# Attention and a gated FFN on one core: another order for the weight steps, the late block, the pairs' first pass and their second steps

## The chip, the cores and the metric

The kernel runs on one core of a Trainium2 chip. The metric is the time of one execution in microseconds of the device. Five engines share the work: TensorE (PE in the profile; PEld is its loading of weights), VectorE (DVE), ScalarE (ACT), GpSimd (POOL) and SyncE (SP). SP does nothing but issue DMAs, one after the other in its own order.

## The reference

Attention inside chunks of 64 positions, for each batch and head, and then a gated feed-forward network over all tokens:

```python
scores = scale * np.matmul(q_c, k_c.transpose(0, 1, 2, 4, 3))      # 64 x 64 in each chunk
attn = np.exp(scores - max) ; attn = attn / (attn.sum + 1e-09)
x = np.matmul(attn, v_c)                                            # as 4608 tokens x 512
g = x @ w_gate ; val = x @ w_val                                    # 512 x 1536 each
out = (g / (1 + np.exp(-g)) * val) @ w_out                          # 1536 x 512
```

There are 8 batches, 8 heads and 576 positions of 64. The inputs q, k, v are float32; the three weights arrive as 64-bit floats and are narrowed on the chip.

## The kernel before, in words

**Tiling.** The 4608 tokens are nine blocks of 512, the 1536 columns twelve steps f of 128. A float32 product is made of three matmuls: each operand is split into an upper and a lower part (`split`: ACT copies the upper, DVE subtracts for the lower), and lower x upper, upper x lower and upper x upper are summed. A step of one block is thus a gate and a value product of 12 matmuls of 128x512 each, Silu of the gate on ACT (`silu`, L490), the product with the value on DVE (`times`, L497), the split of that h (`parts`), and the projection (`project`, L516 to L518) of four row tiles with three matmuls each, summed over all f in four banks of PSUM (`ps_o`). `lag` holds a projection back by one step.

**Stages.** *Opening* (0 to 47 us): attention and the first step of blocks 0 and 1 (a0, a1), a written-out list. *Weight steps* f = 1 to 10 (47 to 196): per step gate and value of a0, the projection of f - 1, gate and value of a1, 60 matmuls. Beside them the weights of the next step are prepared: `Up` for gate and value weights, `Out` for output weights, by `scale` and `below` on ACT and `shift`, `power`, `weigh`, `join` on DVE; `Quarters` forms sums of the up weights for the pairs (`sums`, and then `upper` and `lower`, a split), and the results are stored to DRAM (`save_w`, `save_o`, `quarters.save`). Block 1's h goes to DRAM as well (`put_off`). *Late part* (196 to 259): f = 11, and then block 1's twelve projections, from h and output weights read back (`prepare`, `out_again`), in the order 0 to 11, with the attention of block 2 beside it (`extra`). *Block 2* (259 to 380): twelve direct steps of 36 matmuls, and behind each a piece (`behind`) of the attention of blocks 3 and 4 or of the quarters of weights 0 and 1 (`redo`). *Pairs* (3,4), (5,6) and (7,8): `both_steps` computes gate and value of both blocks by seven products of 6 matmuls in place of eight (`seventh`, L952; factors are the quarters and weights read back by `load_weights`) and the first block's projections, one row tile at each `turn_of`; `second_steps` then makes the second block's twelve projections of 12 matmuls. Behind them stands the attention of the next pair: scores, `exponents` and `normalize`, `turn` (transposes on DVE), `load_v`, `values`, and the next pair's operands `x0` to `x6`.

**Order.** On PE, ACT and DVE the instructions run as the code is written (`manual_schedule`, L543). On SP that holds up to the end of f = 11 (`loading`); from there the scheduler chooses the order of the DMA issues. A tile name with a tag has a fixed place: a new tile of the same tag waits until the old one's readers are done. Output weights read back share the three places of `wp`.

## Time and profile before

| | us |
|---|---|
| median of 3 runs | 980.46 (979.53 to 981.21) |
| the profiled execution | 979.93 |
| its span | 978.1 |
| PE busy in it | 915.6 |
| DVE busy | 550.2 |
| ACT busy | 367.7 |
| moved by DMA | 221.17 MB |

A row of waits names the engine and tile that waited, then what ended the wait, then total us, count and the longest. In a timeline a row begins with its time and its length in us; a bracket gives the idle time ahead of it and what ended it. In the issues the last column is the us from issue to landing.

### The profile page before, as it was taken

What the parts mean: (1) busy time and instruction counts of PE and PEld (TensorE: products, weight loads), DVE (VectorE), ACT (ScalarE), POOL (GpSimd) and SP (SyncE); (2) the same over time, 40 slices, a digit from 0 to 9 for tenths busy, and PEclk for the clock granted to TensorE, in tenths of its full rate; (3) what the DMA queues carried; (4) which work ended last, traced back from release to release, by engine and by line L of the source; (5) the groups of instructions that cost most, each with busy time, mean ns of one, the idle gap of its engine ahead of it and who ended that gap; (6) DMA issues with size and microseconds to landing.
All of it is one profiled execution on the core that took longest, in us unless ns stands there. A gap on an engine that the chain in (4) does not pass through costs nothing.

```text
span 978.1 us, 14802 instructions
## 1 busy us (share of the span) xinstructions
PE 915.6 (94%) x6083; PEld 746.8 (76%) x6083; DVE 550.2 (56%) x863; ACT 367.7 (38%) x561; POOL 6.1 (1%) x14
## 2 busy tenths in 40 slices
PE   7998898887979999999999889999999899999988
PEld 6877677776867877878877668788787688888876
DVE  6976776753377576567586252685673533333332
ACT  4754454441432324342333433423424342222222
POOL 1100000000000000000000000000000000000000
PEclk9999999998998999999999999999999899999999
DMA  9678677769672554765555875656557556555345
GB/s 360 251 293 299 259 253 299 269 237 318 237 220 97 167 211 162 275 242 219 193 200 214 289 252 188 243 215 237 203 208 228 171 200 239 214 215 212 134 151 172
DMA packets 73315, 221.17 MB, mean 226 GB/s; under 512 B 30752, under 2 KB 31008, under 8 KB 59552
## 3 DMA queue, kind: packets, MB, share of 16 engines
q1 hardware_dynamic: 71520, 217.08, 61.8%
q10 hardware_dynamic: 1728, 3.15, 0.9%
q8 instruction: 48, 0.79, 0.3%
q14 instruction: 19, 0.16, 0.0%
HBM read 176.16 MB, written 44.04 MB: 225 GB/s over the span
## 4 chain that ended last, share of the span: by engine, by line
PE 62%; ACT 5%; DVE 5%; DMA 4%; issue 3%; SPq 1%; DVEq 0%; ACTq 0%
PE ps_a L952 20%; PE ps_gv L952 14%; PE ps_o L516 7%; PE ps_o L517 7%; PE ps_o L518 7%; PE ps_gv L461 4%; DMA both<-o 2%; DVE turned L338 1%; PE ps_a L273 1%; ACT s_sb L294 1%; DMA v_t<-in_v 1%; DVE hl L65 1%; ACT hh L64 1%; SPq L255 1%; ACT x L64 1%
## 5 line engine op out<-in xcount | busy, mean ns | idle before, releaser
L952 PE MATMUL ps_a<-x,factors 128*128 128x512 f32 x864 | 220.4, 390 | 5.1 <-ACT h L973 5.1
L516 PE MATMUL ps_o<-both,hl 128*128 128x512 f32 x432 | 173.1, 401 | 22.7 <-DMA both<-o 14.4
L952 PEld LDWEIGHTS ps_a<-x,factors 128*128 128x128 f32 x864 | 161.5, 188 | 40.6 <-ACT h L973 7.2
L461 PE MATMUL ps_gv<-xh,w 128*128 128x512 f32 x576 | 180.2, 397 | 0.0
L517 PE MATMUL ps_o<-both,hh 128*128 128x512 f32 x432 | 170.8, 395 | 0.0
L518 PE MATMUL ps_o<-both,hh 128*128 128x512 f32 x432 | 170.6, 395 | 0.0
L952 PE MATMUL ps_gv<-x,factors 128*128 128x512 f32 x648 | 164.8, 390 | 0.0
L952 PEld LDWEIGHTS ps_gv<-x,factors 128*128 128x128 f32 x648 | 121.3, 188 | 26.5 <-issue 1.5
L461 PE MATMUL ps_gv<-xl,w 128*128 128x512 f32 x288 | 114.5, 404 | 19.9 <-ACT h L490 18.1
L461 PEld LDWEIGHTS ps_gv<-xh,w 128*128 128x128 f32 x576 | 110.8, 192 | 23.4 <-ACT xh L591 0.2
L516 PEld LDWEIGHTS ps_o<-both,hl 128*128 128x128 f32 x432 | 82.7, 191 | 44.4 <-issue 11.6
L65 DVE TENSOR_TENSOR hl<-h,hh 128x512 fp32r<-128x512 f32 x96 | 65.7, 688 | 82.2 <-ACT hh L64 82.2
L64 ACT CAST hh<-h 128x512 fp32r<-128x512 f32 x96 | 58.9, 616 | 106.2 <-PE ps_o L518 59.9
L518 PEld LDWEIGHTS ps_o<-both,hh 128*128 128x128 f32 x432 | 82.7, 191 | 17.8
L517 PEld LDWEIGHTS ps_o<-both,hh 128*128 128x128 f32 x432 | 83.0, 192 | 16.9
L338 DVE STREAM_TRANSPOSE turned<-s_sb 32x256 f32<-32x256 f32 x192 | 83.7, 436 | 2.5
L461 PEld LDWEIGHTS ps_gv<-xl,w 128*128 128x128 f32 x288 | 55.3, 192 | 36.1 <-ACT h L490 22.7
L956 DVE TENSOR_TENSOR h<-h,ps_gv 128x512 f32<-128x512 f32 x36 | 24.7, 687 | 102.9 <-PE ps_gv L952 97.8
L497 DVE SCALAR_TENSOR_TENSOR h<-v,h 128x512 f32<-128x512 f32 x72 | 49.8, 692 | 43.9 <-ACT h L990 39.8
L990 ACT ACTIVATE h<-ps_a 128x512 f32<-128x512 f32 x36 | 21.5, 598 | 110.9 <-PE ps_a L952 110.9
L981 ACT ACTIVATE h<-h 128x512 f32<-128x512 f32 x36 | 22.8, 632 | 75.0 <-DVE h L956 75.0
L490 ACT ACTIVATE h<-ps_gv 128x512 f32<-128x512 f32 x36 | 21.4, 595 | 60.7 <-PE ps_gv L461 60.7
(99 smaller groups left out, 725.8 us busy)
## 6 DMA issues: line engine op xcount, KB each, us to landing
both<-o SPq DMA_DIRECT2D x96, 512.0 KB, 4.9
factors<-w SPq DMA_DIRECT2D x36, 1024.0 KB, 4.8
factors<-t SPq DMA_DIRECT2D x36, 1024.0 KB, 6.2
w<-w SPq DMA_DIRECT2D x12, 1024.0 KB, 4.9
t<-th SPq DMA_DIRECT2D x12, 1024.0 KB, 6.4
raw<-in_wgv SPq DMA_DIRECT2D x11, 1024.0 KB, 10.3
qk_t<-in_qk SPq DMA_DIRECT2D x10, 1024.0 KB, 7.4
out<-o_sb SPq DMA_DIRECT2D x35, 256.0 KB, 3.2
```

The lines of the kernel that those rows point to most:

```text
L64: nc.scalar.copy(out=hi, in_=src)
L65: (engine or nc.vector).tensor_tensor(out=lo, in0=src, in1=hi.bitcast(F32), op=ALU.subtract)
L338: nc.vector.transpose(out=self.turned[to:to + 32, p:p + 2, j, :, 32 * (i % 2):32 * (i % 2) + 32], in_=src[32 * i:32 * i + 32, :, o // 2, 3 ...
L461: nc.tensor.matmul(ps, w, x, start=first and (k, i) == which[0], stop=last and (k, i) == which[-1])
L497: nc.vector.scalar_tensor_tensor(out=h, in0=pv, scalar=2.0 ** -8, in1=h, op0=ALU.mult, op1=ALU.mult)
L516: nc.tensor.matmul(o, hl[:, ts], woh, start=f == 0, stop=False)
L517: nc.tensor.matmul(o, hh[:, ts], wol, start=False, stop=False)
L518: nc.tensor.matmul(o, hh[:, ts], woh, start=False, stop=f == NF - 1)
L952: nc.tensor.matmul(ps, w[:, u, k], x[:, v, k], start=first and k == 0 and n == 0, stop=k == NK // 2 - 1 and n == 2, skip_group_check=True)
L956: nc.vector.tensor_tensor(out=t, in0=t, in1=ps, op=ALU.add)
L981: nc.scalar.activation(h, h, AF.Silu, scale=2.0 ** -8)
L990: nc.scalar.activation(h2, ps1, AF.Silu, scale=2.0 ** -8)
```

## The change

*Weight steps.* `sums` stands behind `join`; the second Silu stands ahead of the quarters' copy and of `scale` of the next output weights; the quarters' lower part behind that. The output weights' store is issued at the step's begin and the quarters' store ahead of the next output weights' load. The quarters of weight 1 are formed at the end of the opening, those of weight 0 in the late part; `redo` is gone. *Late part.* Block 1's last two steps (10 and 11) are not put off to DRAM but projected first (`a1.steps`); the others follow, their output weights in five places in turn, two of them the tags wo0 and wo1. *Output weights in DRAM* lie two steps together, so that one transfer (`out_of_two`) brings two. *Pairs.* In steps 1, 5, 8 and 11 (`bursts`) only the first row tile is projected inside; five products run behind each other, then a row tile, scores or values, and the last two row tiles. Exponents stand in the middle of steps 2 and 6. The sums of `x1`, `x2`, `x5` become steps of their own (`s1`, `s2`, `s4`, `s5`). v1 and v2 lie in one tile under the tags ts and wo1. *Second steps.* All weights are asked for at once, steps 2 to 9 two by two; the next pair's factors are loaded behind step 6 and step 10, and both `values` lie in `both_steps`.

```diff
-            wo_raw.append(const.tile([P, DM], F32, name="wo", tag=f"wo{self.f % 4}"))
+            wo_raw.append(const.tile([P, 2, DM], F32, name="wo", tag=f"wo{self.f % 2}")[:, 0])
...
-        kept_o[f] = store.tile([P, 2, DM], F32, name=f"o{f}")
+        if f % 2 == 0:
+            o = store.tile([P, 2, 2, DM], F32, name=f"o{f}")
+            kept_o[f], kept_o[f + 1], two_o[f // 2] = o[:, 0], o[:, 1], o
         out_now[f] = both
         return both[:, 0], both[:, 1]
...
-    def out_again(f):
-        both = wp.tile([P, 2, DM], F32R, name="both", tag="wo")
+    def out_again(f, pool=wp, tag="wo"):
+        both = pool.tile([P, 2, DM], F32R, name="both", tag=tag)
         nc.sync.dma_start(out=both.bitcast(F32), in_=kept_o[f])
         return both[:, 0], both[:, 1]
...
+    def out_of_two(f, tag):
+        two = const.tile([P, 2, 2, DM], F32R, name="two", tag=tag)
+        nc.sync.dma_start(out=two.bitcast(F32), in_=two_o[f // 2])
+        return [(two[:, i, 0], two[:, i, 1]) for i in range(2)]
...
-            nc.tensor.matmul(o, hl[:, ts], woh, start=f == 0, stop=False)
+            nc.tensor.matmul(o, hl[:, ts], woh, start=f == a.steps[0], stop=False)
...
-            nc.tensor.matmul(o, hh[:, ts], woh, start=False, stop=f == NF - 1)
-            if f == NF - 1:
+            nc.tensor.matmul(o, hh[:, ts], woh, start=False, stop=f == a.steps[1])
+            if f == a.steps[1]:
...
     o.join()
+    quarters = Quarters(1)
+    quarters.sums(w.t)
     p0 = parts(a0, 0, h0)
     wo_f = out_weights(0)
     lag(p0, wo_f)
     down[1].load()
     down[1].scale()
...
+    quarters.upper()
+    quarters.lower()
...
     for f in range(1, NF - 1):
         w, o = up[f + 1], down[f]
+        save_o(f - 1)
         if f + 2 < NF:
             up[f + 2].load()
-        save_o(f - 1)
+        quarters.save()
         down[f + 1].load()
-        if quarters:
-            quarters.save()
         quarters = Quarters(f + 1)
         h0 = gate(a0, f)
...
         w.lower()
-        quarters.sums(w.t)
         o.weigh()
         o.join()
+        quarters.sums(w.t)
         if f + 2 < NF:
             up[f + 2].scale()
-        down[f + 1].scale()
-        quarters.upper()
         wo_f = out_weights(f)
         lag(p0, wo_f)
+        h1 = gate(a1, f)
+        quarters.upper()
+        down[f + 1].scale()
         quarters.lower()
-        h1 = gate(a1, f)
         pv1 = value(a1, f)
...
+    def fetch_h(i):
+        if i < NF // 2 - 1:
+            h = ld.tile([P, 2, N], F32, name="h_in", tag="qk_t")
+            nc.sync.dma_start(out=h, in_=kept_h[i])
+            late.append(h)
     def prepare(f):
-        if f % 2 == 0:
-            h = ld.tile([P, 2, N], F32, name="h_in", tag="qk_t")
-            nc.sync.dma_start(out=h, in_=kept_h[f // 2])
-            late.append(h)
-        p = parts(a1, f, late[-1][:, f % 2])
-        return p, out_again(f)
+        p = parts(a1, f, late[f // 2][:, f % 2])
+        if f % 2:
...
+    ready_o = []
+    def fetch_o(n):
+        while len(ready_o) < min(n, NF - 2):
+            f = len(ready_o)
+            ready_o.append(out_again(f, const, f"wo{f % 5 - 1}") if f % 5 in (1, 2) else out_again(f))
...
-    wo_f = out_weights(f)
+    last_o, wo_f = wo_f, out_weights(f)
     lag(p0, wo_f)
+    a1.steps = f - 1, f - 2
+    put = [(parts(a1, f - 1, h1), last_o)]
     nxt.less_top(nxt.products([nxt.load_qk(2, 2, const, "turned")]), 2)
     h1 = gate(a1, f)
-    put = [prepare(0)]
+    fetch_h(0)
+    fetch_o(1)
     lag(None, None)
-    put.append(prepare(1))
+    fetch_h(1)
+    fetch_o(2)
     save_o(f - 1)
-    quarters.save()
-    save_o(f)
     pv1 = value(a1, f)
     times(h1, pv1)
-    put_off(h1)
+    put.append((parts(a1, f, h1), wo_f))
     loading.__exit__(None, None, None)
...
     nxt.places()
-    extra = {0: lambda: nxt.exponents(0), 1: lambda: (nxt.exponents(2), sums(0)), 2: lambda: nxt.normalize(0, z[0]),
-             3: lambda: (sums(2), load_v()), 4: lambda: nxt.normalize(2, z[2]), 6: turn, 7: lambda: copy(2),
-             8: columns, 9: lambda: (first(2), rest(0)), 10: lambda: rest(2)}
+    extra = {0: lambda: (nxt.exponents(0), quarters.save()), 1: lambda: (nxt.exponents(2), sums(0)), 2: lambda: nxt.normalize(0, z[0]),
+             3: lambda: (sums(2), load_v()), 4: lambda: nxt.normalize(2, z[2]), 5: lambda: (q0.sums(q0.again()), q0.upper()),
+             6: lambda: (turn(), q0.lower(), q0.save()), 7: lambda: copy(2), 8: columns, 9: lambda: (first(2), rest(0)), 10: lambda: rest(2)}
+    save_o(NF - 1)
     for f in range(NF):
         lag(*put.pop(0))
+        fetch_o(f + 3)
         extra.get(f, lambda: None)()
         if f + 2 < NF:
-            put.append(prepare(f + 2))
+            put.append((prepare(f), ready_o[f]))
...
+        def s1(self):
             self.sum = ld.tile([P, NK // 2 * N], F32, name="sum", tag="qk_t")
             nc.vector.tensor_tensor(out=self.sum, in0=self.quarter(1, 0), in1=self.quarter(1, 1), op=ALU.add)
+        def x1(self):
             self.halves(1, self.sum)
...
+    def turns(which):
+        if pending:
+            project(*pending[0], which=which)
+            if T - 1 in which:
+                pending.pop()
...
             wo_f = out_again(f)
-            h = gated_pair(pair, f, kept[-1][:, f % 2])
+            h = gated_pair(pair, f, kept[-1][:, f % 2], [0] if f in bursts else range(T),
+                           middle.get(f, nothing))
             p = parts(pair.a[0], f, h)
+            if f in bursts:
+                turns([1])
+                bursts[f]()
+                turns([2, 3])
...
-            lag(p, wo_f)
-            if not (pair.last and f + 2 >= NF):
-                load_weights((f + 2) % NF)
...
     def second_steps(pair, behind, nothing=lambda: None):
-        put = [(parts(pair.a[1], f, pair.kept[f // 2][:, f % 2]), out_again(f)) for f in range(2)]
+        def prepare(f):
+            return parts(pair.a[1], f, pair.kept[f // 2][:, f % 2])
+        wo_f = [out_again(0), out_again(1)]
+        for f in (2, 4, 6, 8):
+            wo_f += out_of_two(f, f"w{6 + f // 2}")
+        put = [prepare(0)]
         for f in range(NF):
-            lag(*put.pop(0))
+            lag(put.pop(0), wo_f[f])
+            if f == 0:
+                wo_f += out_again(10), out_again(11, const, "wo0")
+            if f + 1 < NF:
+                put.append(prepare(f + 1))
             behind.get(f, nothing)()
-            if f + 2 < NF:
-                put.append((parts(pair.a[1], f + 2, pair.kept[(f + 2) // 2][:, f % 2]), out_again(f + 2)))
+            if not pair.last and f in (6, 10):
+                load_weights(f // 10)
...
     a, pair = nxt, Pair(3, "w2")
     c = pair.a[0]
-    first = {0: Quarters(0), 1: Quarters(1)}
-    def redo(f):
...
-    behind = {0: lambda: (redo(0), scores(c, False)), 1: lambda: (softmax_and_turn(c, 0), redo(1)),
+    behind = {0: lambda: scores(c, False), 1: lambda: softmax_and_turn(c, 0),
               2: lambda: (softmax_and_turn(c, 1), softmax_and_turn(c, 2)),
-              3: lambda: (softmax_and_turn(c, 3), load_v(c)), 4: lambda: values(c), 5: lambda: scores(pair.second(), False),
-              6: lambda: softmax_and_turn(pair.a[1], 0),
+              3: lambda: (softmax_and_turn(c, 3), load_v(c)), 4: lambda: (values(c, False), pair.x0(), pair.x3()),
+              5: lambda: scores(pair.second(), False), 6: lambda: softmax_and_turn(pair.a[1], 0),
               7: lambda: (softmax_and_turn(pair.a[1], 1), softmax_and_turn(pair.a[1], 2)),
               8: lambda: (softmax_and_turn(pair.a[1], 3), load_v(pair.a[1]), load_weights(0)),
-              9: lambda: (values(pair.a[1]), pair.x0(), pair.x1()), 10: lambda: (pair.x2(), pair.x3()),
-              11: lambda: (pair.x4(), pair.x5(), load_weights(1), pair.x6())}
+              9: lambda: (values(pair.a[1], False), pair.s1(), pair.x1(), pair.s4()),
...
-                      3: lambda: (softmax_and_turn(c, 1), softmax_and_turn(c, 2)), 4: lambda: softmax_and_turn(c, 3),
-                      6: lambda: scores(n.second()), 7: lambda: softmax_and_turn(n.a[1], 0),
-                      8: lambda: (softmax_and_turn(n.a[1], 1), softmax_and_turn(n.a[1], 2)),
-                      9: lambda: (softmax_and_turn(n.a[1], 3), load_v(c))}
-            later = {0: lambda: values(c), 1: lambda: (load_v(n.a[1]), n.x0()), 3: lambda: (values(n.a[1]), n.x1()),
-                     4: lambda: n.x2(), 6: lambda: n.x3(), 7: lambda: n.x4(), 8: lambda: n.x5(), 10: lambda: n.x6()}
-        both_steps(pair, behind)
+            bursts = {1: lambda: scores(c), 5: lambda: scores(n.second()), 8: lambda: values(c),
+                      11: lambda: values(n.a[1])}
+            middle = {2: lambda: c.exponents(0, NP), 6: lambda: n.a[1].exponents(0, NP)}
+            behind = {2: lambda: c.normalize(0, NP), 3: lambda: (softmax_and_turn(c, 1), softmax_and_turn(c, 2)),
+                      4: lambda: softmax_and_turn(c, 3), 6: lambda: (n.a[1].normalize(0, NP), load_v(c)),
+                      7: lambda: (softmax_and_turn(n.a[1], 1), softmax_and_turn(n.a[1], 2)),
+                      8: lambda: (softmax_and_turn(n.a[1], 3), load_v(n.a[1]))}
+            later = dict(enumerate((n.x0, n.s1, n.x1, n.s4, n.s2, n.x2, n.x3, n.x4, n.s5, n.x5, n.x6)))
+        both_steps(pair, middle, behind, bursts)```

PE's, ACT's and DVE's instructions are the same in number and shape. Three places, as the program orders them.

ACT in a weight step, before (raw is a loaded weight, ts and th the quarters, wo and both the output weights):

```order
L84 ACTIVATE t<-raw 128x1024
L84 ACTIVATE wo<-raw 128x512
L172 CAST th<-ts 128x1024
L64 CAST both<-wo 128x512
L490 ACTIVATE h<-ps_gv 128x512 x2
L555 DMA h_736<-h 128x512
```

and after:

```order
L84 ACTIVATE t<-raw 128x1024
L64 CAST both<-wo 128x512
L500 ACTIVATE h<-ps_gv 128x512
L172 CAST th<-ts 128x1024
L84 ACTIVATE wo<-raw 128x512
L500 ACTIVATE h<-ps_gv 128x512
L565 DMA h_969<-h 128x512
```

The first Silu and the split of the output weights now stand ahead of the quarters' copy and of the scaling of the next output weights.

SP at the start of the first pair's second steps, before (o_711, o_783 and o_896 are the output weights of steps 0, 1 and 2; factors the next pair's):

```order
L477 DMA both<-o_1909 128x1024
L943 DMA factors<-w_2373 128x2048
L943 DMA factors<-t_2443 128x2048
L477 DMA both<-o_711 128x1024
L943 DMA factors<-w_2533 128x2048
L943 DMA factors<-t_2601 128x2048
L477 DMA both<-o_783 128x1024
L477 DMA both<-o_896 128x1024
```

and after (o_715 is that of steps 0 and 1, o_899 to o_1560 those of 2 to 9, two by two, o_1777 that of 10 and 11):

```order
L481 DMA both<-o_1777 128x1024
L487 DMA two<-o_899 128x2048
L487 DMA two<-o_1119 128x2048
L481 DMA both<-o_715 128x1024
L487 DMA two<-o_1339 128x2048
L487 DMA two<-o_1560 128x2048
L255 DMA v_t<-in_v 128x4x64
L257 DMA v_t<-in_v 64x4x64 x2
L255 DMA v_t<-in_v 128x4x64
L257 DMA v_t<-in_v 64x4x64 x2
L247 DMA qk_t<-in_qk 128x2x1024
L481 DMA both<-o_715 128x1024
```

The factors are gone from ahead of the output weights, and the second load from o_715, that of step 1, stands behind six loads of v and one of q and k.

PE in the step of a pair that has scores, from the second row tile on, before:

```order
L952 MATMUL ps_gv<-x,factors 128x512 x6
L516 MATMUL ps_o<-both,hl 128x512
L517 MATMUL ps_o<-both,hh 128x512
L518 MATMUL ps_o<-both,hh 128x512
L952 MATMUL ps_a<-x,factors 128x512 x6
L516 MATMUL ps_o<-both,hl 128x512
L517 MATMUL ps_o<-both,hh 128x512
L518 MATMUL ps_o<-both,hh 128x512
L273 MATMUL ps_a<-qk_t 64x64 x64
```

and after:

```order
L988 MATMUL ps_a<-x,factors 128x512 x6
L988 MATMUL ps_gv<-x,factors 128x512 x6
L988 MATMUL ps_a<-x,factors 128x512 x6
L988 MATMUL ps_gv<-x,factors 128x512 x6
L988 MATMUL ps_a<-x,factors 128x512 x6
L526 MATMUL ps_o<-both,hl 128x512
L527 MATMUL ps_o<-both,hh 128x512
L528 MATMUL ps_o<-both,hh 128x512
L275 MATMUL ps_a<-qk_t 64x64 x64
```

The row tiles that stood between the products stand behind them, and the scores have a row tile ahead of them and two behind.

56 lines of the change are left out of this document (29 added, 27 removed).

## The prediction

> **What bounds the kernel now.** I read the page first, then busy time by stage, then TensorE's waits stage by stage, then single waits in the timeline. The page's span and its first part:
>
> ```profile
> span 978.1 us, 14802 instructions
> PE 915.6 (94%) x6083; PEld 746.8 (76%) x6083; DVE 550.2 (56%) x863; ACT 367.7 (38%) x561; POOL 6.1 (1%) x14
> ```
>
> TensorE (PE) is the bound, and its instructions are the same in number and shape after the change. So only the 62 us in which it stands, and what a stand costs afterwards, can move. Two stages by busy time:
>
> ```profile
> core 0: us, PE busy (x) PEld busy (x) DVE busy (x) ACT busy (x) POOL busy (x), PEclk, DMA share, GB/s
> 47.00:196.00 149.00, 135.83 (x581) 109.06 (x579) 107.93 (x166) 72.18 (x97) 0.00 (x0) 0.99 0.74 278
> 786.00:936.00 150.00, 149.89 (x660) 123.84 (x660) 49.35 (x74) 45.42 (x78) 0.00 (x0) 1.00 0.52 193
> ```
>
> The last pair's first pass (second row) has no stand at all, at a granted clock of 1.00: a denser program is not clocked down. The waits of PE in seven windows, in this order: 47 to 196 (first row), 196 to 259 (next two), 259 to 380 (three), 380 to 536 (one), 536 to 585 (three), 741 to 786 (three), 786 to the end (last):
>
> ```profile
> PE ps_gv L461 <- ACT h L490: 12.6, 9, 2.6
> PE ps_o L516 <- DMA both<-o: 6.8, 1, 6.8
> PE ps_o L516 <- DVE z L427: 1.6, 1, 1.6
> PE ps_gv L461 <- ACT h L490: 4.9, 1, 4.9
> PE ps_gv L461 <- ACT s_sb L281: 1.8, 1, 1.8
> PE ps_a L351 <- DVE h L497: 1.5, 1, 1.5
> PE ps_a L952 <- ACT h L973: 3.5, 3, 1.8
> PE ps_o L516 <- DMA both<-o: 5.4, 2, 3.4
> PE ps_a L351 <- DMA v_t<-in_v: 1.7, 2, 1.4
> PE ps_o L516 <- DVE hl L65: 1.3, 1, 1.3
> PE ps_o L516 <- DVE hl L65: 2.7, 2, 1.3
> PE ps_o L516 <- DMA both<-o: 2.2, 1, 2.2
> PE ps_a L351 <- DMA v_t<-in_v: 1.5, 2, 0.8
> PE ps_o L516 <- ACT o_sb L531: 1.2, 1, 1.2
> ```
>
> What a wait costs beyond its idle time shows in PE's timeline of one weight step:
>
> ```profile
> 84.48 0.61 PE L461 MATMUL ps_gv<-xh,w 128*128 128x512 f32 x2
> 87.71 0.53 PE L461 MATMUL ps_gv<-xl,w 128*128 128x512 f32 x1 [2.61 <-ACT h L490]
> 88.04 1.05 PE L461 MATMUL ps_gv<-xh,w 128*128 128x512 f32 x2
> ```
>
> Two matmuls take 0.61 us warm and 1.05 behind this wait. One starts each 0.227 us (0.61 less one 0.39 row), 0.43 in the slow stretch; eight at half rate add 1.6 us, and the refill 0.16 to every wait. Counted so in PE's timeline, 8 matmuls of the weight stage run at half rate, 7 of the late part, 19 of block 2, 15 of pair 1's second steps and 10 of pair 2's, each 0.2 us lost.
>
> A page of the Trainium skill differs here: "TensorE: Matmul & The Clock Gate", Part 1, lets the clock fall after an idle window of about 3.4 us. The trace does not agree, since 2.61 us was enough. By the page's rule the new 2.1 us wait below would cost no half rate, and the forecast would be 0.8 us lower.
>
> **The change part by part.** *Weight steps, f = 1 to 10.* One step of a sum is 60 matmuls, 13.6 us of PE. In the step around that wait, ACT's timeline, and then DVE's:
>
> ```profile
> 83.01 0.68 ACT L84 ACTIVATE wo<-raw 128x512 f32<-128x512 f32 x1 [2.31 <-DMA raw<-in_wo]
> 85.59 1.04 ACT L172 CAST th<-ts 128x1024 fp32r<-128x1024 f32 x1 [1.91 <-DMA t<-th]
> 87.06 0.59 ACT L490 ACTIVATE h<-ps_gv 128x512 f32<-128x512 f32 x1
> ```
>
> ```profile
> 81.76 0.69 DVE L165 TENSOR_TENSOR ts<-t 128x512 f32<-128x512 f32 x1
> 83.73 0.69 DVE L102 TENSOR_TENSOR wo<-wo,o_sb 128x512 f32<-128x512 f32 x1
> 87.80 1.22 DVE L175 TENSOR_TENSOR th<-ts,th 128x1024 fp32r<-128x1024 f32 x1
> ```
>
> The Silu that frees PE's bank (87.06) stands behind two instructions that wait for transfers, the load of the next output weights and the store of the last quarters. After the change it stands before both, behind only the split of the output weights. The three quarter sums begin at 81.76 and fill, with a 0.4 us product, the 2.0 us to join at 83.73; behind join, they let it start at 82.2 and end at 82.9. Split 0.6, Silu 0.6: done by 84.2, and PE wants the bank at 84.9 (end of the 84.48 row). Margin 0.7 us. DVE then does sums (1.5), the split's lower part (0.7), the quarters' lower part (1.22) and the product of the other block (0.7), to about 87.4 with hand-overs, where PE asks for that at 84.9 + 12 x 0.227 = 87.6. Margin 0.2: next to nothing, and if lost it comes back each step. Gain: 13.2 us idle (with one of 0.6 at 196), ten refills, one half rate: 16.4.
>
> Against it: the quarters of weight 1 now stand in the opening on DVE, ahead of the product that PE's value product waits for:
>
> ```profile
> 42.55 0.68 DVE L65 TENSOR_TENSOR hl<-h,hh 128x512 fp32r<-128x512 f32 x1
> 43.94 0.68 DVE L497 SCALAR_TENSOR_TENSOR h<-ps_gv,h 128x512 f32<-128x512 f32 x1
> 45.09 0.39 PE L461 MATMUL ps_gv<-xl,w 128*128 128x512 f32 x1
> ```
>
> Sums 1.5 ahead of 42.55 and the lower part 1.1 ahead of 43.94 end the product at 47.1 instead of 44.6; the value product starts at 47.2 instead of 45.09: 2.1 us lost, and 0 to 1.6 of half rate (I take 0.8). The transfers of the stage:
>
> ```profile
> DMA packets 8120, 41.48 MB, mean 278 GB/s; under 512 B 829, under 2 KB 829, under 8 KB 4655
> raw<-in_wgv SPq DMA_DIRECT2D x7, 1024.0 KB, 10.3
> ```
>
> With one more store of 1 MB the same bytes must pass in some 137 us: 310 GB/s instead of 278. The up weights are now loaded behind the store of the output weights, at the step's begin; landing after 7 to 10.3 us, they are wanted once hh is split and hurt when they come after 10.6, as their scaling (1.1) must end where the output weights' split begins (82.9 less 71.3, the step's start 60 x 0.227 ahead of 84.9). I take 1.8 us over ten steps (0 if they land in 7, about 13 if each is 1.3 late). Sum: 16.4 - 2.1 - 0.8 - 1.8 = **11.7 gained**.
>
> *Late part of block 1.* Steps 10 and 11 come first, their operands at hand, so 2 x 2.72 us of PE cover the loads; the next weights go to two more places and no longer wait for a slot. Both waits go: 6.8 + 1.6 + 0.3 refill + 1.5 half rate = **10.2**. The splits then run 0.2 us ahead of PE, so I bound this by 7 and 10.2.
>
> *Block 2.* The redone quarters leave ACT's queue. In ACT's timeline:
>
> ```profile
> 291.80 1.04 ACT L172 CAST th<-ts 128x1024 fp32r<-128x1024 f32 x1 [8.11 <-issue]
> ```
>
> This copy waited for DVE sums and held the Silu behind the 4.9 us wait; the 1.8 us wait had the other copy ahead of it. They go: 4.9 + 1.8 + 0.3 + 3.8 half rate = 10.8. Factors prepared earlier shorten the 1.8 us wait at 383 (one of the three on L973), 1.8 more. But DVE loses the stand in which it caught up: two steps of turning take 7.2 + 1.4 us on DVE each against 8.2 on PE, so the columns at step 4 will wait as those at step 9 do (1.5): -1.7. Sum **10.9**.
>
> *Both steps of pairs 1 and 2.* Exponents move behind the last copy of a step: two waits of 0.8 each go, 2.0 a pair with refill. But steps 5 and 8 run five products without a projection between them, each behind a step of turning on DVE. PE's first product of such a step, and DVE in it:
>
> ```profile
> 447.22 1.52 PE L952 MATMUL ps_a<-x,factors 128*128 128x512 f32 x6
> ```
>
> ```profile
> 448.58 7.18 DVE L338 STREAM_TRANSPOSE turned<-s_sb 32x256 f32<-32x256 f32 x16
> 456.40 0.68 DVE L956 TENSOR_TENSOR v<-v,ps_a 128x512 f32<-128x512 f32 x1
> ```
>
> With the step's start at 447.2 the add at 456.40 ends at +9.9 and frees the bank of the last product. With three projections of 0.68 and six products of 1.36 ahead PE asks at +10.2; with one projection, at +8.8: a new wait of 1.1, two a pair. Net **0.2 lost** a pair; between 2 gained (if the turning is done earlier) and 3 lost.
>
> *Second steps.* No next factors are loaded ahead of the output weights, eight of these wait in four tiles, v is loaded long before, the evictions stand ahead of the second split. Pair 1: 5.4 + 1.7 + 1.3, refills 1.1, half rate 3.0: 12.5. Pair 2: 2.7 + 2.2 + 1.5, refills 1.5, half rate 2.1: 10.0. Last pair: 1.2 + 0.2. In pair 1, though, step 1's weights are queued on SP behind the next pair's v (six issues) and 1 MB of q and k:
>
> ```profile
> 547.17 0.55 SPq L253 DMA_DIRECT2D v_t<-in_v  x1
> 547.77 1.25 SPq L255 DMA_DIRECT2D v_t<-in_v  x2
> ```
>
> One v tile takes 1.9 us to issue, two 3.9, from the middle of the columns, some 2.4 us before the first projection; then 0.4 for q and k, and the weights' transfer, 4 to 7 us behind 1 MB (10.3 for the up weights is the far end). It lands at 6 to 9 where PE wants it at 5.4: 0.6 to 3.6 late, with half rate 0 to 1.6; I take 4.0, near the far end, as transfers crowd there. So 8.5 + 10.0 + 1.4.
>
> Sum: 11.7 + 10.2 + 10.9 - 0.2 - 0.2 + 8.5 + 10.0 + 1.4 = 52.3. The profiled execution took 979.93 (span 978.1); less 52.3 it is 927.6, and with the median of the runs (980.46, 0.5 above it) **928.0 us**.
>
> **Rivals.** (a) *Transfers pace the weight steps.* For: 10.3 us for the up weights is at the edge of 10.6. Against: 278 GB/s take a share of 0.74, so 310 take 0.83. If each load lands 1.3 us or more too late, most of the 11.7 is lost: 928 + 12 = 940.
> By "DMA: Bandwidth & Descriptors", Bandwidth, of the Trainium skill, 1 MB transfers run at 341 GB/s; an odd step's 4.75 MB would then take 14.6 us, an estimate, 1.0 over PE's 13.6, five times: 5 us in place of 1.8, or 931. The trace speaks against so low a ceiling: 278 GB/s at a share of 0.74 make 375 at a full one.
> (b) *Stalls move instead of going*: bursts wait 2 us in place of 1.1, pair 1 stands 7 in place of 4, DVE's margin of 0.1 turns into 0.5 a step: 4 + 3 + 5 = 12 more, 940. For: the margins; against: PE's first pass over the last pair shows that such steps can run full.
> (c) *All goes well*: no slip, no half rate, no new waits: 52.3 + 2.6 + 1.7 + 4 + 4 = 64, 915.
> (d) *Slower*: SP issues in order, and the up weights now stand behind a store that waits for DVE at the very end of a step. If that store slips by one load time (10.3 us) each step, each of ten steps grows by some 7 us beyond today's; from 5.2 us a step it outweighs the 52. Time 980 - 52 + 70 + 12 = 1010. Against: the store's source is ready where the step ends, at a period of 13.6.
> (e) *The change doesn't do what it says*: the named releasers are wrong and waits stay: 970.
>
> **How the numbers follow.** Forecast 0.58, (a) 0.14, (b) 0.14, (c) 0.06, (d) 0.04, (e) 0.04. Likeliest's own range 921 to 937; with (a), (b) and most of (c) 914 to 947. A measurement of this kernel tells about 0.2% (2 us) from no change. Faster: all but (d) and a little of (e): 0.94; within 0.2%: 0.02; slower: 0.04.
>
> **What would show it.** Right: no wait on the Silu line in the weight stage, PE dense from 205 to 250, no redone quarters in block 2, one new wait near 45, one of about 1.1 in steps 5 and 8 of pairs 1 and 2, one on output weights early in pair 1's second steps. Wrong: waits for the up weights' load or on the first product of each weight step, or PE busy well below 97%.

## The result

The changed kernel takes 928.43 us (median of 4 runs, 928.03 to 928.85), the kernel before, run beside it, 980.0 us. The ratio is 0.9475, with a 95% interval of 0.9458 to 0.9491. The forecast was 928.0 us. That the total fits so well is partly luck: two terms that came out larger than forecast and two that came out smaller cancel, as the table below shows. One of the five executions of the kernel with several edits together, below, fell into a slower state of the chip (996.08 us at a granted clock of 0.85) and is left out of that kernel's figures.

The page of the profile after, span and first part:

```profile
span 925.8 us, 14786 instructions
PE 898.9 (97%) x6083; PEld 739.8 (80%) x6083; DVE 549.4 (59%) x862; ACT 371.0 (40%) x561; POOL 6.0 (1%) x14
```

TensorE has the same 6083 matmuls. It is busy 16.7 us less, some 10 of it because 8 of them run at half rate where the prediction counted 59 at 0.2 us each, and it stands 36 us less. (VectorE's instructions are not the same in number, but one fewer: the quarters of weight 1 are formed before the weight is split, which saves one addition of 1.2 us.) Busy time by stage, after (the windows go from the first matmul of a stage to that of the next; weight steps, late part, block 2, first pair's steps for both, its second steps, the second pair's two stages, the last pair's first):

```profile
core 0: us, PE busy (x) PEld busy (x) DVE busy (x) ACT busy (x) POOL busy (x), PEclk, DMA share, GB/s
42.10:180.00 137.90, 136.97 (x602) 112.43 (x601) 114.17 (x176) 75.76 (x101) 0.00 (x0) 1.00 0.89 325
180.00:236.80 56.80, 53.88 (x478) 43.49 (x477) 30.86 (x50) 23.10 (x36) 0.00 (x0) 1.00 0.87 296
236.80:348.40 111.60, 107.79 (x946) 89.05 (x945) 74.49 (x122) 36.65 (x51) 0.00 (x0) 1.00 0.54 174
348.40:502.50 154.10, 152.28 (x1024) 125.36 (x1023) 97.34 (x161) 58.10 (x90) 0.00 (x0) 1.00 0.64 230
502.50:547.00 44.50, 39.35 (x283) 32.14 (x282) 22.93 (x26) 19.55 (x29) 0.00 (x0) 0.92 0.74 256
547.00:701.00 154.00, 152.17 (x1023) 125.42 (x1022) 94.54 (x159) 56.42 (x88) 0.00 (x0) 1.00 0.61 220
701.00:738.30 37.30, 37.30 (x284) 30.90 (x283) 23.05 (x26) 19.56 (x29) 0.00 (x0) 1.00 0.69 236
738.30:884.20 145.90, 145.90 (x645) 120.82 (x644) 47.72 (x71) 43.25 (x74) 0.00 (x0) 1.00 0.57 215
```

Of these windows only the first pair's second steps have a granted clock below 1.00. PE's waits after, in these windows: the weight steps (two rows), the late part (two), block 2 (two), the first pair's steps for both (one), its second steps (one), the stretch from 738 us to the end (last row); the second pair's steps for both read as the first's, and its second steps have none:

```profile
PE ps_gv L463 <- ACT h L500: 0.7, 1, 0.7
PE ps_gv L463 <- DVE h L507: 0.2, 1, 0.2
PE ps_o L526 <- DVE hl L65: 1.4, 1, 1.4
PE ps_o L526 <- DMA both<-o: 1.4, 1, 1.4
PE ps_a L353 <- DVE h L507: 3.0, 2, 1.5
PE ps_a L275 <- DMA qk_t<-in_qk: 0.8, 1, 0.8
PE ps_a L988 <- DVE v L992: 1.8, 2, 0.9
PE ps_o L526 <- DMA both<-o: 5.1, 1, 5.1
PE ps_o L526 <- DVE hl L65: 1.3, 1, 1.3
```

Stage by stage, from first matmul to first matmul (a pair's two stages are taken together, since one set of values moved from the one into the other):

| stage | before, us | after, us | change | forecast |
|---|---|---|---|---|
| opening and weight steps | 194.7 | 178.6 | -16.1 | -11.7 |
| late part | 63.5 | 56.9 | -6.6 | -10.2 |
| block 2 | 120.7 | 111.6 | -9.1 | -9.1 |
| first pair | 206.7 | 198.6 | -8.1 | -10.1 |
| second pair | 202.0 | 191.2 | -10.7 | -9.8 |
| last pair and end | 185.2 | 183.7 | -1.5 | -1.4 |

(The forecast's 10.9 for block 2 held 1.8 for a wait that lies, by these boundaries, in the first pair.)

### The profile page after: what moved, and what is told of

The parts are those of the page before. It is cut to its first block, busy times and chain, and to the rows that moved or that the text cites. A ratio compares the mean times of both kernels' runs of the same rounds, so it can differ in the third digit from the quotient of the medians.

```text
span 925.8 us, 14786 instructions
## 1 busy us (share of the span) xinstructions
PE 898.9 (97%) x6083; PEld 739.8 (80%) x6083; DVE 549.4 (59%) x862; ACT 371.0 (40%) x561; POOL 6.0 (1%) x14
## 4 chain that ended last, share of the span: by engine, by line
PE 78%; DVE 13%; DMA 4%; ACT 2%; issue 2%; SPq 0%; POOL 0%; ACTq 0%; DVEq 0%; POOLq 0%
PE ps_a L988 20%; PE ps_gv L463 15%; PE ps_gv L988 14%; PE ps_o L526 9%; PE ps_o L528 9%; PE ps_o L527 9%; DVE turned L340 5%; PE ps_a L275 2%; DMA both<-o 1%; DVE h L507 1%; PE ps_a L353 1%; DVE hl L65 1%; DMA two<-o 1%; DMA o<-both 1%; DMA qk_t<-in_qk 1%
## 5 line engine op out<-in xcount | busy, mean ns | idle before, releaser
L988 PE MATMUL ps_a<-x,factors 128*128 128x512 f32 x864 | 219.9, 390 | 3.7 <-DVE v L992 3.7
L988 PEld LDWEIGHTS ps_a<-x,factors 128*128 128x128 f32 x864 | 161.8, 188 | 39.0 <-DVE v L992 5.3
L463 PE MATMUL ps_gv<-xh,w 128*128 128x512 f32 x576 | 176.0, 390 | 0.2 <-ACT xh L601 0.2
L988 PE MATMUL ps_gv<-x,factors 128*128 128x512 f32 x648 | 164.4, 389 | 0.0
L526 PE MATMUL ps_o<-both,hl 128*128 128x512 f32 x336 | 133.4, 397 | 9.4 <-DMA both<-o 6.5
L988 PEld LDWEIGHTS ps_gv<-x,factors 128*128 128x128 f32 x648 | 121.6, 188 | 25.3
L527 PE MATMUL ps_o<-both,hh 128*128 128x512 f32 x336 | 131.6, 392 | 0.0
L528 PE MATMUL ps_o<-both,hh 128*128 128x512 f32 x336 | 131.6, 392 | 0.0
L463 PEld LDWEIGHTS ps_gv<-xh,w 128*128 128x128 f32 x576 | 108.1, 188 | 22.6 <-ACT xh L601 0.4
L65 DVE TENSOR_TENSOR hl<-h,hh 128x512 fp32r<-128x512 f32 x98 | 67.5, 690 | 76.3 <-ACT hh L64 76.2
L463 PE MATMUL ps_gv<-xl,w 128*128 128x512 f32 x288 | 111.4, 393 | 0.9 <-ACT h L500 0.7
L64 ACT CAST hh<-h 128x512 fp32r<-128x512 f32 x98 | 60.4, 618 | 115.9 <-PE ps_o L528 58.7
L992 DVE TENSOR_TENSOR h<-h,ps_gv 128x512 f32<-128x512 f32 x36 | 24.7, 687 | 109.3 <-PE ps_gv L988 109.1
L526 PEld LDWEIGHTS ps_o<-both,hl 128*128 128x128 f32 x336 | 63.6, 189 | 25.0 <-issue 7.8
L528 PEld LDWEIGHTS ps_o<-both,hh 128*128 128x128 f32 x336 | 63.5, 189 | 13.5
L507 DVE SCALAR_TENSOR_TENSOR h<-v,h 128x512 f32<-128x512 f32 x72 | 49.8, 692 | 40.7 <-ACT h L1032 36.2
L527 PEld LDWEIGHTS ps_o<-both,hh 128*128 128x128 f32 x336 | 63.6, 189 | 12.7
L463 PEld LDWEIGHTS ps_gv<-xl,w 128*128 128x128 f32 x288 | 53.9, 188 | 13.6 <-ACT h L500 1.5
L1032 ACT ACTIVATE h<-ps_a 128x512 f32<-128x512 f32 x36 | 21.5, 598 | 103.4 <-PE ps_a L988 103.4
L992 DVE TENSOR_TENSOR v<-v,ps_a 128x512 f32<-128x512 f32 x36 | 24.7, 687 | 37.5 <-PE ps_a L988 34.8
```

Of the source, the lines that this page charges most:

```text
L64: nc.scalar.copy(out=hi, in_=src)
L65: (engine or nc.vector).tensor_tensor(out=lo, in0=src, in1=hi.bitcast(F32), op=ALU.subtract)
L463: nc.tensor.matmul(ps, w, x, start=first and (k, i) == which[0], stop=last and (k, i) == which[-1])
L507: nc.vector.scalar_tensor_tensor(out=h, in0=pv, scalar=2.0 ** -8, in1=h, op0=ALU.mult, op1=ALU.mult)
L526: nc.tensor.matmul(o, hl[:, ts], woh, start=f == a.steps[0], stop=False)
L527: nc.tensor.matmul(o, hh[:, ts], wol, start=False, stop=False)
```

## The experiments

Each run changes the kernel after, unless it says otherwise. Where a wait in its own stage decides, the trace is read; the totals carry a fraction of a per cent of noise.

### The order on ScalarE and VectorE in the weight loop, undone and done alone

```diff
-        o.weigh()
-        o.join()
         quarters.sums(w.t)
+        o.weigh()
+        o.join()
         if f + 2 < NF:
             up[f + 2].scale()
+        down[f + 1].scale()
+        quarters.upper()
         wo_f = out_weights(f)
         lag(p0, wo_f)
-        h1 = gate(a1, f)
-        quarters.upper()
-        down[f + 1].scale()
         quarters.lower()
+        h1 = gate(a1, f)
         pv1 = value(a1, f)
```

> The changed kernel with one thing undone: in the weight loop the sums, the quarters' copy, the scaling of the next output weights and the second Silu stand as before; the stores and loads keep the new order. Theory (the order on ScalarE and VectorE is the cause of the weight stage's gain): the ten waits on the Silu come back, 13 us of idle time and 1.5 us of refills, with up to 1.6 us of half rate: 941 to 945 us in place of 928.4. Rival (the new order of the stores frees the quarters' tile and brings the raw weights early enough, so that the Silu would no longer stand long behind them): at most five of the waits, none over 0.8 us, 928 to 933 us.

949.22 us, ratio to before 0.9697 (0.9669 to 0.9725): 20.8 us more than the changed kernel, beyond the range of the theory (941 to 945 us) and far from the rival's. The same lines exchanged the other way in the kernel before:

> The kernel before with that one thing done: the new order of these instructions on ScalarE and VectorE in the weight loop, stores and loads as before. Theory: the order suffices, the waits on the Silu go: 980.0 less 13 to 16.4, 964 to 967 us. Rival (without the earlier stores the copy of the quarters or the lower part is late and the waits only move): less than 6 us gained, 974 to 980 us.

964.19 us, ratio 0.9856 (0.9822 to 0.989), inside the theory's range. PE's waits between 42 and 200 us, of the kernel with the order undone (first row) and of the one with the order alone (second):

```profile
PE ps_gv L463 <- ACT h L500: 15.5, 10, 4.4
PE ps_gv L461 <- DVE h L497: 2.5, 4, 0.6
```

The order of these instructions is the cause of the Silu waits. It is needed, and alone it brings about 16 of the 52 us. Undoing it costs more than that, most of all by a wait of 4.4 us in step 1, where before it was 0.6. A load of output weights is issued there behind the store of the quarters of weight 1. It lands at 58.4, about as in the changed kernel (58.9), but with the old order the Silu stands behind it. ACT's timeline in step 1 of the kernel with the order undone:

```profile
58.44 0.66 ACT L84 ACTIVATE wo<-raw 128x512 f32<-128x512 f32 x1 [5.05 <-DMA raw<-in_wo]
59.01 1.03 ACT L172 CAST th<-ts 128x1024 fp32r<-128x1024 f32 x1
59.94 0.61 ACT L64 CAST both<-wo 128x512 fp32r<-128x512 f32 x1
60.46 0.59 ACT L500 ACTIVATE h<-ps_gv 128x512 f32<-128x512 f32 x1
```

With the order alone, four waits of 0.6 us are left, on VectorE's product. The next run tells where they come from.

### The order of the weight loop's DMA issues undone

```diff
-        save_o(f - 1)
         if f + 2 < NF:
             up[f + 2].load()
-        quarters.save()
+        save_o(f - 1)
         down[f + 1].load()
+        quarters.save()
```

> The changed kernel with the order of the DMA issues in the weight loop as before: load of the up weights, store of the output weights, load of the next output weights, store of the quarters. Theory (the transfers of this stage are covered by a step of 13.6 us in either order, as no wait on a load shows after the change): 927.5 to 930 us, no wait over 0.5 us between 47 and 180 us. Rival (the store of the quarters ahead of the load is what keeps the quarters' tile free): the copy waits for the store again, lower part and product come late, 0.5 to 1.5 us a step, 933 to 943 us.

931.52 us, ratio 0.9518 (0.9487 to 0.9549), between the two expected ranges. The weight steps take 141.3 us in place of 137.9, and beside the two waits of the changed kernel they have four of 0.5 to 0.7 us on the product again, one every other step. SP's issues in such a step, then ACT and VectorE:

```profile
76.44 0.38 SPq L224 DMA_DIRECT2D raw<-in_wo  x1
76.91 0.42 SPq L179 DMA_DIRECT2D t<-th  x1
```

```profile
85.53 1.05 ACT L172 CAST th<-ts 128x1024 fp32r<-128x1024 f32 x1 [1.47 <-DMA t<-th]
```

```profile
86.61 1.23 DVE L175 TENSOR_TENSOR th<-ts,th 128x1024 fp32r<-128x1024 f32 x1 [1.58 <-ACT th L172]
87.76 0.68 DVE L507 SCALAR_TENSOR_TENSOR h<-ps_gv,h 128x512 f32<-128x512 f32 x1
```

The store of the quarters is issued behind the load of the next output weights, which every other step waits for its place until 76.4. The store then lands at 85.4, and the copy of the next quarters, which writes the same tile, waits 1.5 us for it. The lower part and the product follow late. In the changed kernel the store of that step is issued at 72.5, and the same product ends at 87.1 in place of 88.4, with PE asking at about 87.6. So the rival's mechanism was right and its price too high: some 0.6 us every other step, not 0.5 to 1.5 in each. The new order of the stores is worth 3 us.

### The second steps as before

```diff
-        wo_f = [out_again(0), out_again(1)]
-        for f in (2, 4, 6, 8):
-            wo_f += out_of_two(f, f"w{6 + f // 2}")
...
+        put = [(parts(pair.a[1], f, pair.kept[f // 2][:, f % 2]), out_again(f)) for f in range(2)]
...
-            if f + 2 < NF:
-                load_weights(f + 2)
+            if not (pair.last and f + 2 >= NF):
+                load_weights((f + 2) % NF)
```

> The changed kernel with the second steps as before: output weights one step at a time through three places, two steps ahead, the next pair's factors loaded in the last two of the steps for both; v loaded early and the values in the steps for both, as changed. Theory (loads of factors ahead of the output weights, and too few places, are the cause of the waits there): the waits on output weights (5.4 and 2.2 us before) and on the lower split (4.0) come back with refills and half rate, about 15 us, and the wait of 5.2 with 2 of half rate and refill in the first pair goes: 932 to 941 us. Rival (v behind everything on the queue was the cause; with v early the rest is covered): 918 to 929 us.

932.24 us, ratio 0.952 (0.9493 to 0.9548): 3.8 us more, at the theory's low end. In its own stages it costs 2.9, 2.1 and 1.6 us over the three pairs, 6.6 in all (the profiled execution is 5.2 us longer; its late part and block 2, which these edits leave alone, came out 1.2 us shorter). PE's waits in the first pair's second steps of this kernel:

```profile
PE ps_o L526 <- DMA both<-o: 5.8, 2, 4.8
PE ps_o L526 <- ACT o_sb L541: 1.2, 1, 1.2
```

The long wait on step 1's weights is there in this kernel as well. It does not come from the new places, and the theory was wrong to let it go. SP issues this load at 510.3 us here, behind six loads of v and one of q and k, as in the changed kernel (rows below). Nor do the old waits on output weights come back as expected: beside the long one there are 1.0 us in the first pair and 0.3 in the second, where the kernel before had 5.4 and 2.2. What comes back in each pair is 1.2 us on an eviction. So the total fits the theory by luck, 6.6 us for these edits and not 15. Of the 18.8 us that pairs 1 and 2 gained these edits carry 5.0. The rest lies in what the run leaves as changed, v, the values and the exponents among it. The run does not tell these apart, so what cured the old waits on output weights stays open.

### Block 1's last steps last again, in five places

```diff
-    a1.steps = f - 1, f - 2
-    put = [(parts(a1, f - 1, h1), last_o)]
...
+    put_off(h1)
...
-            put.append((prepare(f), ready_o[f]))
+            put.append((prepare(f + 2), ready_o[f + 2]))
```

(The h of both steps goes to DRAM by `put_off`.)

> The changed kernel with block 1's last two steps put off to DRAM again and projected last, the output weights still in five places. Theory (the two steps whose operands are at hand cover the loads that the others wait for): without them the first projections wait for h and output weights again, 5 to 9 us more, 933 to 938 us, the wait in the first 12 us of the late part. Rival (the two further places alone are the cure, the order does nothing): 927 to 930 us.

933.24 us, ratio 0.9524 (0.9509 to 0.9539): 4.8 us more, at the low end of the theory's range. The late part takes 60.5 us in place of 56.9. PE's waits in it:

```profile
PE ps_o L526 <- DMA both<-o: 5.5, 1, 5.5
```

The weights of the second projection land at 207.4 us, 5.5 after PE asks. Two more places alone do not bring the early output weights in time; the two steps whose operands are at hand cover them.

### Two pieces of the late part moved

```diff
     nxt.less_top(nxt.products([nxt.load_qk(2, 2, const, "turned")]), 2)
+    save_o(f - 1)
+    save_o(f)
     h1 = gate(a1, f)
...
-    save_o(f - 1)
...
-             5: lambda: (q0.sums(q0.again()), q0.upper()), 6: lambda: (turn(), q0.lower(), q0.save())
+             6: turn
-    save_o(NF - 1)
+    q0_work = {5: lambda: q0.sums(q0.again()), 6: q0.upper, 7: lambda: (q0.lower(), q0.save())}
...
             put.append((prepare(f), ready_o[f]))
+        q0_work.get(f, lambda: None)()
```

(Here and in the run after it, only the entries of `extra` that change are shown.)

> The changed kernel with two pieces of the late part moved: the stores of the last two output weights are issued before block 1's last gate, and the quarters of weight 0 are formed in three pieces behind the split of the steps 5, 6 and 7 in place of ahead of it in 5 and 6. Theory: the wait of 1.35 us on an output weight near 213 us comes from the store of step 11's weights, which lands at 208.6 and ahead of which the queue does not issue the next load; the wait of 1.44 near 222 comes from the quarters' sums ahead of the split on VectorE. Both go, 2.8 us and two refills: late part 53.5 to 54.5 us in place of 56.9, total 925 to 926 us. Rival (three places of five are held by steps 9 to 11, and the transfers' rate sets the pace): the first wait moves to the next load, at most 1.6 us gained, 926.8 us or more.

926.03 us, ratio 0.9451 (0.9437 to 0.9466), and a late part of 54.5 us in place of 56.9, both at the upper end of the theory's ranges. The wait on the split is gone: it was the quarters of weight 0, which stood ahead of the split. Of the other wait the rival's mechanism was right: it moved. PE's one wait left in the late part of this kernel, 6 us earlier than that of the changed kernel:

```profile
PE ps_o L526 <- DMA both<-o: 1.1, 1, 1.1
```

The store that held the queue was moved (in the changed kernel it lands at 208.6 us, and SP issues the next load at 208.7), and a load that stands earlier took over the wait, 1.1 us in place of 1.4.

### The quarters of weight 0 back in block 2

```diff
-             5: lambda: (q0.sums(q0.again()), q0.upper()), 6: lambda: (turn(), q0.lower(), q0.save())
+             6: turn
...
-    behind = {0: lambda: scores(c, False),
+    behind = {0: lambda: (q0.sums(q0.again()), q0.upper(), q0.lower(), q0.save(), scores(c, False)),
```

> The changed kernel with the quarters of weight 0 formed behind step 0 of block 2, ahead of the scores, as before, in place of the late part; those of weight 1 stay in the opening. Theory (the copy waits for VectorE's sums and holds the Silu behind it): the late part loses its wait of 1.4 us, block 2 gets one of 1.8 us or more on the Silu or on the scores' maxima with half rate behind it, 930.5 us, 929.5 to 932. Rival (one copy fits there, only two were too many): 926.5 to 927.5 us.

929.3 us, ratio 0.9487 (0.9466 to 0.9509), just below the theory's range and not told from the changed kernel by its total. The stages show both halves: the late part loses its wait on the split (55.4 us, with one of 2.0 on output weights left), and block 2 gets back the old one (113.4 us), without half rate. PE's wait in block 2, and what ACT does ahead of the copies that end it:

```profile
PE ps_gv L463 <- ACT s_sb L283: 1.8, 1, 1.8
```

```profile
245.38 1.04 ACT L172 CAST th<-ts 128x1024 fp32r<-128x1024 f32 x1 [1.58 <-DVE ts L167]
246.33 1.07 ACT L283 COPY s_sb<-ps_a 128x512 f32<-128x512 f32 x2
```

The copy waits for the sums in the late part and in block 2 alike, and whatever is behind it on ScalarE waits with it. (The other set's wait of 4.9 us was not brought back by any run.)

### Step 1's output weights in a free place

```diff
-        wo_f = [out_again(0), out_again(1)]
+        wo_f = [out_again(0), out_again(1, const, "wo0")]
...
-                wo_f += out_again(10), out_again(11, const, "wo0")
+                wo_f += out_again(10), out_again(11)
```

> The changed kernel with the output weights of a pair's second step 1 loaded to a place of their own that is free through the steps for both, and those of step 11 to one of the three in turn. Theory (in the first pair this load waits for its place and is then queued behind six loads of v and one of q and k; nothing else is late there): the wait of 5.2 us near 517 us goes with 1.6 of half rate and the refill, 7.0 us, 921.4 us; the first pair's second steps take 37.2 to 38 us as the second pair's, in place of 44.6. Rival (transfers crowd there, whatever is asked for last is late): the wait moves to the weights of steps 10 or 11, 925 us or more.

919.71 us, ratio 0.9383 (0.9366 to 0.9401), 8.7 us less than the changed kernel where 7.0 was expected. The first pair's second steps have no wait at all:

```profile
503.07:540.30 37.23, 37.23 (x284) 30.86 (x282) 22.99 (x26) 19.56 (x29) 0.00 (x0) 1.00 0.87 308
```

They last 37.2 us, as the second pair's, 7.3 less than in the changed kernel, where SP issues this load as the last of these rows:

```profile
504.25 0.38 SPq L255 DMA_DIRECT2D v_t<-in_v  x1
504.69 1.73 SPq L257 DMA_DIRECT2D v_t<-in_v  x2
506.52 0.69 SPq L255 DMA_DIRECT2D v_t<-in_v  x1
507.25 1.77 SPq L257 DMA_DIRECT2D v_t<-in_v  x2
509.13 1.34 SPq L247 DMA_DIRECT2D qk_t<-in_qk  x1
510.66 0.34 SPq L481 DMA_DIRECT2D both<-o  x1
```

### The bursts, shortened in two steps and taken away

```diff
-            h = gated_pair(pair, f, kept[-1][:, f % 2], [0] if f in bursts else range(T),
+            h = gated_pair(pair, f, kept[-1][:, f % 2], ([0, 1, 2] if f in (5, 8) else [0]) if f in bursts else range(T),
...
+                if f not in (5, 8):
+                    turns([1])
                 bursts[f]()
-                turns([2, 3])
+                turns([3] if f in (5, 8) else [2, 3])
```

> The changed kernel with the bursts of steps 5 and 8 of pairs 1 and 2 shortened: row tiles 0, 1 and 2 are projected inside again and only the last stands behind the scores or the values; steps 1 and 11 stay. Theory (the wait of 0.9 us in each of these steps is the bank that VectorE frees late, behind the turning, and two row tiles of 0.68 us ahead of the product cover it): four waits of 0.91 and their refills go, 4.3 us, 924 us. Rival (the row tiles are missed behind the products: the scores or the columns then wait for evictions): as much is lost there, 927 to 930 us.

927.56 us, ratio 0.9467 (0.9447 to 0.9486), in the rival's range. The four waits of 0.9 us on the bank go, and four of 0.4 us come, the rival's. PE's waits in the second pair's steps for both:

```profile
PE ps_a L275 <- ACT h L1032: 0.4, 1, 0.4
PE ps_a L353 <- ACT h L1032: 0.4, 1, 0.4
```

The scores and the values directly behind the last product wait for its Silu. And in the first pair's second steps the wait for step 1's weights grew to 7.2 us. Then without any burst, with the scores or values behind the fourth row tile in all four steps:

```diff
-            h = gated_pair(pair, f, kept[-1][:, f % 2], [0] if f in bursts else range(T),
+            h = gated_pair(pair, f, kept[-1][:, f % 2], range(T),
...
-                turns([1])
                 bursts[f]()
-                turns([2, 3])
```

> The changed kernel without bursts: in steps 1, 5, 8 and 11 of pairs 1 and 2 all row tiles are projected inside, and the scores or values stand behind the last of them; exponents in the middle of steps 2 and 6 stay. Theory (the bursts' only cost is the bank freed late, 4 waits of 0.9 us, and three row tiles cover it): 924 us, no wait near 421, 461, 619 and 659 us. Rival (what stood behind the products covered the scores' and values' banks): waits of 0.4 to 1 us appear at the scores and values of all eight steps, 926 to 931 us.

917.36 us, ratio 0.9369 (0.9346 to 0.9392): 11.1 us less than the changed kernel, far more than the 4.3 expected, and neither rival. In the steps for both of pairs 1 and 2 PE has no wait left over 0.15 us. And the wait of 5.1 us in the first pair's second steps is gone too, in a kernel that touches nothing of them. SP's issues there:

```profile
503.11 0.32 SPq L481 DMA_DIRECT2D both<-o  x1
503.80 0.38 SPq L255 DMA_DIRECT2D v_t<-in_v  x1
```

Step 1's weights are now issued ahead of v, some 7 us earlier than in the changed kernel. This load waits for a place in `wp` that a projection frees: the last matmul that it waits for is done at 503.1. In the burst of step 11 the last two row tiles of the projection stand behind the products and the values, so the place comes free late, and SP has the loads of v in front. That the place decides fits the run above, in which a free one had the same effect. From first matmul to first matmul the first pair is 8.7 us shorter than in the changed kernel and the second 1.9, together 10.6 of the 11.1.

### What the runs point to, together

The late part's two pieces, the free place, two output weights of the late part asked for before the last split (`fetch_o(2)` ahead of `out_weights(f)`), and in steps 5 and 8 row tiles 0 and 1 inside, 2 behind the last product and 3 behind the scores or values:

> The changed kernel with these edits together: step 1's weights in the free place (step1_free), the two pieces of the late part moved (late_two), the first two output weights of the late part asked for before the last output weights are split, and in steps 5 and 8 of pairs 1 and 2 the row tiles 0 and 1 inside, the third behind the last product and the fourth behind the scores or values. Theory (each wait has a cause of its own, so the gains add): 928.4 less 7.3 (second steps), less 2.4 and 1.3 (late part), less 4 x 0.7 (bank of the last product) is 914.6 us, 913 to 916.5. Rival (a wait that goes is given back at the next late transfer): 917 us or more.

913.76 us (median of four runs), ratio to the kernel before 0.9337 (0.9313 to 0.9361), 14.7 us less than the changed kernel; the theory's 914.6 holds. The profiled one of the four took 917.56; it has a gap of 1.0 us at 430 that the profile puts down to no wait, and 0.9 us more on q and k in block 2, and the cause of both is open. The late part has no wait of over 0.3 us and takes 53.1 us, the second steps of pairs 1 and 2 take 37.2 each. The waits on the bank are down to what the margin leaves, here the second pair's:

```profile
PE ps_a L990 <- DVE v L994: 0.5, 2, 0.2
```

These edits and the run without bursts were not tried together. The last run adds a move of the quarters of weight 1, out of the opening into step 1:

```diff
-    quarters.upper()
-    quarters.lower()
...
-        quarters = Quarters(f + 1)
+        first, quarters = quarters, Quarters(f + 1)
...
         w.upper()
+        if f == 1:
+            first.upper()
...
         o.join()
+        if f == 1:
+            first.lower()
+            first.save()
         quarters.sums(w.t)
```

> The same, and the upper and lower parts of the quarters of weight 1 moved from the end of the opening into step 1, behind the split of its weights, with their store. Theory (the new wait of 0.7 us near 45 us is the copy that stands ahead of the Silu on ScalarE, not the product on VectorE): the wait goes, 0.85 us, and 0.4 near 59: 1.2 us below the other kernel of this call. Rival (step 1 has no room left on VectorE, margin 0.2): a wait of 0.5 to 1 us comes near 59 us, no gain.

920.43 us, ratio 0.9397 (0.9378 to 0.9417): 6.7 us worse than without it, beyond the rival. ACT's timeline at the end of step 1:

```profile
62.35 1.04 ACT L172 CAST th<-ts 128x1024 fp32r<-128x1024 f32 x1 [6.04 <-DMA t<-th]
63.30 0.66 ACT L84 ACTIVATE wo<-raw 128x512 f32<-128x512 f32 x1
63.86 0.58 ACT L500 ACTIVATE h<-ps_gv 128x512 f32<-128x512 f32 x1
```

The wait near 45 us became 0.8 us on the product. The new one has nothing to do with VectorE's room: the store of these quarters is issued 10 us later than before and lands at 62.3, and the next quarters need the tile. It is the mechanism of the stores once more, with a longer delay.

## Why the prediction was right, point by point

**Weight steps: mechanism right, three terms too dark.** The Silu behind two instructions that wait for transfers was the cause (runs with the order undone and alone). The margin of 0.2 us for VectorE's product was right: it shows as one wait of 0.2 us near 59, and is gone as soon as a store is 4 us later. Wrong was the new wait near 45. I put it on the product on VectorE at 2.1 us and 0.8 of half rate. That product ends at 46.9, as forecast to 0.2 us, but PE starts at 45.7. The value product of step 1 now takes the bank of the gate product before it, which the Silu frees at 45.6, and the Silu stands behind the copy of the new quarters. (In the kernel before, the same product started at 45.09 and its Silu only at 45.29, so there it had another bank: the row was read rightly, but the bank changed.) The wait is 0.7 us, with no half rate. The 1.8 us for late transfers did not come: the up weights land in 6.9 us (10.3 before), where the forecast put 0 for 7. What I did not see is that the earlier store of the quarters is itself a part of the gain, 3 us, without which the margin would not hold.

**Rival (a), transfers, came close.** The weight stage moves 325 GB/s at a DMA share of 0.89, where I had 310 and 0.83. A step, and another stretch of the same length, after:

```profile
97.50:111.10 13.60, 13.60 (x62) 11.26 (x61) 11.13 (x18) 7.52 (x10) 0.00 (x0) 1.00 0.96 340
158.50:172.10 13.60, 13.60 (x62) 11.26 (x61) 11.13 (x18) 7.52 (x10) 0.00 (x0) 1.00 0.99 404
```

The step moves 340 GB/s at a share of 0.96, with PE full. "DMA: Bandwidth & Descriptors", Bandwidth, of the Trainium skill gives 341 GB/s for 1 MB transfers. The trace does not show that as a ceiling: the second stretch moves 404 GB/s at a share of 0.99, with PE full as well, and the 1 us a step that I worked out from it was not lost. My reading that a full share would make 375 does not hold either: at nearly the same share these two rows differ by 64 GB/s.

**Late part: too bright.** Both old waits went, but I priced nothing in their place. The step that failed is "the next weights go to two more places and no longer wait for a slot": a load also stands behind what SP has in front of it. One was issued only at 208.7, when a store had landed, and PE waited 1.4 us for it. The quarters of weight 0, which I only took out of block 2, cost 1.4 us where they were put. 6.6 us in place of 10.2, outside the bound of 7.

**Block 2: right to a tenth.** The two waits on the redone quarters went, and the new one at the values of step 4 came with 1.5 us, as that of step 9. The run with one set of quarters back in block 2 gives the old 1.8 us back; the other set's 4.9 us were not tested apart.

**Steps for both: right in size.** The two waits of 0.8 us a pair are gone with the exponents' new place. The forecast had a new wait of 1.1 us in steps 5 and 8 of pairs 1 and 2. It is 0.91 us, 1.07 with the refill, four times. Not seen was that a burst also frees the place of the output weights later.

**Second steps: the queue was right, its price and the gain's cause were not.** Step 1's weights behind v and q and k were forecast at 4.0 us and cost 7.2: 5.15 of wait, 8 matmuls at half rate, and refill. Counted from the first projection as the forecast did (507.0 us), the load was issued at 3.6, not 1.9, as the loads of v took 4.8 us to issue in place of 3.9 and that of q and k 1.3 in place of 0.4. It took 7.0 us and landed at 10.6, beyond the 6 to 9 forecast. These 3.2 us more than explain the first pair's gap between 10.1 and 8.1; the rest of that pair was 1.2 us better than forecast. Apart from that wait both pairs gained some 1 us more than forecast, but the factors out of the way and the four tiles, named as causes, carry 5.0 us of it (the run with the second steps as before). The second pair's 0.9 us was not followed.

The time lies within 0.5 us of the forecast because +4.4 and +0.9 stand against -3.6 and -2.0. Rivals (c), (d) and (e) did not come. Of the three terms of (b), stalls that move, one did: the first pair's wait cost 7.2, as its 7 in place of 4. The bursts' waits were 0.9 and not 2, and VectorE's margin held. Of the signs, PE dense from 205 to 250 failed with the two waits of the late part, at 214 and 223; the others came, but for a wait of 0.7 us on the Silu near 45, where one on the product was meant.

## What to carry to other kernels

On an engine that works in order, put the instruction that frees the bottleneck's bank ahead of every instruction that waits for a transfer, and count the price of a moved piece at the place where it lands as well as where it leaves. A tile that is stored and then written again is free when its store lands, so a store's place on the issue queue belongs to the tile's next writer: one run lost 0.6 us every other step by it, another 5 us at once. Before bunching work on the bottleneck, look at what each moved instruction releases: here the bursts cost some 4 us where they stand, and 7 more a stage later, through one place that came free late.

## What the runs showed of the hardware

The half rate after a wait is not a matter of the wait's length alone. In PE's timelines of these runs, no wait of 1.0 to 1.8 us before a 128x512 matmul is followed by a stretch of matmuls at half rate, each of the 17 waits of 3.4 us and more is, for 6 to 13 matmuls, and of the 17 waits between 1.83 and 2.61 us, 6 are and 11 are not. Two of the kernel with the order undone, the same instruction after waits of 2.05 and 2.06 us:

```profile
123.56 0.50 PE L463 MATMUL ps_gv<-xl,w 128*128 128x512 f32 x1 [2.05 <-ACT h L500]
123.89 0.62 PE L463 MATMUL ps_gv<-xh,w 128*128 128x512 f32 x2
...
153.94 0.78 PE L463 MATMUL ps_gv<-xl,w 128*128 128x512 f32 x1 [2.06 <-ACT h L500]
154.52 1.05 PE L463 MATMUL ps_gv<-xh,w 128*128 128x512 f32 x2
```

"TensorE: Matmul & The Clock Gate", Part 1, of the Trainium skill, with an idle window of about 3.4 us, agrees with the waits above it; what decides between 1.83 and 2.61 us no run here tells.
